# Unnormalised tap diagonals, a later request of chunk 1, and a split evacuation in the start-up of a fused convolution and gated MLP kernel

## The chip, the cores and the metric

The kernel runs on one core of one Trainium2 chip. The metric is device time in microseconds (us). Where runs are compared with each other, they were run in the same rounds on the same chip as the kernel before.

Engine names in the profile: PE is TensorE (PEld its weight loads), ACT is ScalarE, DVE is VectorE, POOL is GpSimd, SP is SyncE. A name with a "q" at the end (SPq, POOLq) is the sequencer of that engine, here issuing a DMA.

Other terms: a tap is one of the seven weights of the convolution, or the operation that applies it. A diagonal is the identity matrix times one tap; with it PE applies that tap in a matmul. A group is 64 of the 192 channels in both batch halves, on 128 partitions. PSUM holds what matmuls write, SBUF the other tiles; an evacuation is the copy from PSUM to SBUF. Fillers are matmuls on zeros whose results nobody reads.

## The reference

```python
# x [8, 4096, 192], weight [8 heads, 7 taps]
w = softmax(weight, axis=-1)                    # per head
x_pad = zeros(6 rows) ++ x                      # causal, along the sequence
conv[b, s, h, g] = sum_k w[h, k] * x_pad[b, s + k, h, g]
# MLP on 32768 tokens: w_in [192, 2048], w_out [2048, 192], beta [2048]
h = conv @ w_in
out = (h * sigmoid(beta * h)) @ w_out           # fp32 out
```

The kernel computes SiLU(beta*h), which is beta times too large, and divides the output weights by beta once, at start-up.

## The kernel before

The sequence is worked in 32 chunks of 1024 tokens (512 tokens in each of two batch halves). In steady state, PE multiplies hidden and output layers without a pause, VectorE computes the convolution of chunk s+2 with seven tap operations, and ScalarE does the SiLU. Only chunks 0 and 1 are handled specially, because nothing has run ahead of them. That start-up is what the change touches.

SyncE issues the loads in this order; `load_x(x1, ...)` is chunk 1, `w_in_raw` are the first 256 columns of the input weights in fp32, needed for the first two hidden tiles:

```python
    for i in range(2):
        load_x(x0, 0, i)                       # chunk 0, two halves
    load_x(x1, TOK, 0)                         # chunk 1, first half
    for r in range(2):
        nc.sync.dma_start(out=w_in_raw[r * DG : (r + 1) * DG], in_=w_in_v[:, :, 0:F0])
    load_x(x1, TOK, 1)                         # chunk 1, second half
    for i in range(NW - 1):
        load_w_out(i)                          # output weights, fp32, slices 0 to 2
    load(2)
    load_w_out(NW - 1)
    load(3)
```

The tap weights, their diagonals (for the convolution of groups 0 and 1 of chunk 0 on PE), and GpSimd's loads of the other input-weight columns. The traces show these loads in the software queue (q0); they cast fp32 to bf16 on the way, and I call them the casting loads. The one-element copy `hold` keeps them back until the taps are ready:

```python
    nc.vector.reduce_max(nmax, pw, axis=mybir.AxisListType.X, negate=True)
    nc.scalar.activation(cw, pw, AF.Exp, bias=nmax, accum_out=total)
    nc.scalar.activation(warm, warm, AF.Silu)
    nc.vector.reciprocal(total, total)
    nc.vector.tensor_scalar_mul(cw, cw, total)
    # ... (cut)
    for b in range(NB):
        cast_rows(nc.vector.tensor_copy, x0b, x0, b)
        if b == 1:
            diags(0, 2)
    hold = setup.tile([1, 1], FP32)
    nc.gpsimd.tensor_copy(hold, cw[0:1, 0:1])
    load_w_in(F0, FW)                          # casting loads, two DMAs each
    for i in range(1, NW):
        load_w_in(i * FW, (i + 1) * FW)
```

The evacuation of the four transposed blocks of chunk 0, and the rest that matters here:

```python
    for b in range(NB):
        # ... transposes of block b into pt (cut)
        (nc.vector.tensor_copy if b == 2 else nc.scalar.copy)(tokens(xt0, b), pt)
        # ... (cut)
    diags(2, 4)
    diags(4, K)
    # ... per group c of chunk 0: seven matmuls; ScalarE casts chunk 1, evacuates
    #     group c, and casts w_in_raw to bf16 after group 0 (cut)
    # ... group 2: five taps on VectorE, two on PE, added (cut)
    scale_w_out(0)                             # output-weight slice / beta, on GpSimd
    scale_w_out(1)                             # GpSimd too; slices 2 and 3 on VectorE
    # ... (cut)
    first_work = {                             # VectorE's work in step u of chunk 0
        4: [None, None],                       # None: one tap operation of chunk 1
        5: [None],
        6: [conv1_evac, lambda: scale_w_out(2), None],
        # ... (cut)
    }
```

## Time and profile before

| | before |
|---|---|
| time, median of the 3 runs at first, of 6 beside the change | 690.03, 690.42 us |
| profiled span | 688.0 us |
| PE busy | 682.2 us |
| first convolution matmul | 7.21 us |
| first hidden matmul | 11.12 us |
| first hidden matmul of chunk 1 | 29.39 us |

The profile page, the line of busy times and the chain of work that ended last:

```profile
PE 682.2 (99%) x11312; PEld 521.1 (76%) x11312; DVE 524.7 (76%) x467; ACT 579.0 (84%) x530; POOL 9.9 (1%) x20
...
PE 98%; DMA 1%; ACT 0%; DVE 0%; issue 0%; ACTq 0%
```

PE is the limit, and the kernel can gain or lose only where PE has to wait: in the first 30 us.

The timeline of the kernel before (start in us, duration in us, engine, source line, operation, output and inputs, count; in brackets the idle time before it and what ended it):

```profile
0.81 1.48 SPq L158 DMA_DIRECT2D x<-in_x_dram  x3
...
2.34 1.31 SPq L169 DMA_DIRECT2D w_in_raw<-in_moe_w_in_dram  x2
...
3.69 0.60 SPq L158 DMA_DIRECT2D x<-in_x_dram  x1
...
4.29 5.24 POOL L211 DMA_DIRECT2D w_in_s<-in_moe_w_in_dram  x8
...
7.68 0.48 DVE L338 TENSOR_SCALAR ct<-xt,cw 128x512 bf16<-128x512 f32 x1
...
9.62 0.83 ACT L332 CAST w_in_s<-w_in_raw 128x768 bf16<-128x768 f32 x1
...
11.12 1.66 PE L424 MATMUL ph<-ct,w_in_s 64*128 64x512 bf16 x12
...
11.42 0.69 DVE L352 TENSOR_TENSOR ct<-pa,ct 128x512 bf16<-128x512 f32 x1
...
15.39 1.69 DVE L338 TENSOR_SCALAR ct<-xt,cw 128x1024 bf16<-128x1024 bf16 x1
...
29.39 0.83 PE L424 MATMUL ph<-ct,w_in_s 64*128 64x512 bf16 x6
```

The last line is my landmark: from there PE runs without a pause, so a shift of this line is a shift of the end.

Two more views of the kernel before. First, the loads of `w_in_raw` alone (issues, and the time from issue to landing); the two DMAs, issued at 2.34 and 3.05, landed at 7.87 and 8.75:

```profile
L169 SPq DMA_DIRECT2D w_in_raw<-in_moe_w_in_dram x2: 597/635/673, 2.3 to 3.1; - x2
...
DMA to landing us min/median/max: 5.5/5.6/5.7
```

### The profile page before, as it was taken

How to read it: one execution, taken by the hardware profiler on the slowest of the kernel's cores; microseconds unless marked ns; L12 is line 12 of the kernel's file. 1: busy time of each engine (PE TensorE's matmuls, PEld its weight loads, DVE VectorE, ACT ScalarE, POOL GpSimd, SP SyncE). 2: the span in 40 equal slices, each digit the busy share in tenths (PEclk: the TensorE clock that was granted, in tenths of full speed). 3: DMA queues.
4: the chain of work that ended last, by engine and by line, in shares of the span. 5: the costliest groups of instructions: out<-in, count | busy, mean ns of one | idle time of the engine just before them, and what ended most of it. 6: DMA issues, size and time to landing. Idle time of an engine off the chain costs nothing.

```text
span 688.0 us, 24344 instructions
## 1 busy us (share of the span) xinstructions
PE 682.2 (99%) x11312; PEld 521.1 (76%) x11312; DVE 524.7 (76%) x467; ACT 579.0 (84%) x530; POOL 9.9 (1%) x20
## 2 busy tenths in 40 slices
PE   8999999999999999999999999999999999999998
PEld 4777777777777777777777777777777777777777
DVE  7989877788777787777797777887777977777712
ACT  7988888888888888888888888888888888888893
POOL 5000000000000000000000000000000000000000
PEclk9999999999999999999999999999999999999999
DMA  9734333244332244332444332444323443322111
GB/s 234 190 97 117 105 100 98 58 107 117 101 99 77 77 116 116 95 99 61 98 117 105 93 97 57 116 117 96 103 60 93 117 109 96 100 59 59 49 36 59
DMA packets 121861, 67.06 MB, mean 97 GB/s; under 512 B 53264, under 2 KB 121760, under 8 KB 121760
## 3 DMA queue, kind: packets, MB, share of 16 engines
q1 hardware_dynamic: 120048, 64.12, 34.7%
q0 software_dynamic: 1664, 1.38, 1.2%
q8 instruction: 88, 1.44, 0.9%
q14 instruction: 13, 0.11, 0.0%
q10 hardware_dynamic: 48, 0.01, 0.0%
HBM read 29.89 MB, written 25.17 MB: 80 GB/s over the span
## 4 chain that ended last, share of the span: by engine, by line
PE 98%; DMA 1%; ACT 0%; DVE 0%; issue 0%; ACTq 0%
PE ph L424 48%; PE pa L457 25%; PE pb L457 24%; DMA x<-in_x_dram 1%; PE pb L287 1%; ACT g L432 0%; PE ph L287 0%; DVE x0b L226 0%; ACT xt L302 0%; PE pa L287 0%; PE pb L233 0%; PE ph L233 0%; DVE diag L260 0%; ACT osb L473 0%; ACT beta L309 0%
## 5 line engine op out<-in xcount | busy, mean ns | idle before, releaser
L432 ACT ACTIVATE g<-ph,beta 128x1024 bf16<-128x1024 f32 x512 | 569.7, 1115 | 94.5 <-PE ph L424 89.8
L457 PEld LDWEIGHTS <-g 64*128 64x128 bf16 x8160 | 370.7, 94 | 102.3 <-issue 0.2
L424 PE MATMUL ph<-ct,w_in_s 64*128 64x512 bf16 x3072 | 424.3, 376 | 0.9 <-ACT g L432 0.9
L340 DVE SCALAR_TENSOR_TENSOR ct<-xt,cw,ct 128x1536 bf16<-128x1536 bf16 (+2 forms) x190 | 336.9, 1773 | 2.5
L457 PE MATMUL pa<-w_out_s,g 64*128 64x192 bf16 x4112 | 244.8, 243 | 0.0
L457 PE MATMUL pb<-w_out_s,g 64*128 64x192 bf16 (+1 forms) x4048 | 230.4, 243 | 0.0
L424 PEld LDWEIGHTS <-w_in_s 64*128 64x128 bf16 x3072 | 159.6, 94 | 54.8 <-issue 2.7
L475 DVE TENSOR_REDUCE osb<-pa 128x384 f32<-128x768 f32 x64 | 61.3, 958 | 122.5 <-PE pa L457 121.1
L475 DVE TENSOR_REDUCE osb<-pb 128x384 f32<-128x768 f32 x63 | 60.3, 957 | 29.1 <-PE pb L457 29.1
L106 DVE CAST xb<-xf 128x768 bf16<-128x768 f32 x60 | 40.5, 677 | 0.0
L338 DVE TENSOR_SCALAR ct<-xt,cw 128x1536 bf16<-128x1536 bf16 (+2 forms) x32 | 32.4, 1011 | 0.0
L473 ACT COPY osb<-pb 128x192 f32<-128x192 f32 x1 | 0.3, 319 | 7.2 <-PE pb L457 7.2
L211 POOL DMA_DIRECT2D w_in_s<-in_moe_w_in_dram x8 | 5.2, 662 | 0.0
L223 PE MATMUL ph<-zeros 128*128 128x512 bf16 (+2 forms) x11 | 4.1, 485 | 1.1 <-DVE warm L180 1.1
L287 PE MATMUL pb<-xt,diag 64*128 64x512 f32 (+1 forms) x21 | 4.7, 443 | 0.0
L121 DVE COPY xt<-xt 128x18 bf16<-128x18 bf16 x27 | 4.4, 164 | 0.0
L287 PEld LDWEIGHTS pb<-xt,diag 64*128 64x128 f32 (+1 forms) x21 | 2.7, 187 | 0.9 <-issue 0.4
L314 POOL TENSOR_TENSOR w_out_s<-w_out_raw,beta_r 128x768 bf16<-128x768 f32 x2 | 3.1, 1564 | 4.1 <-DVE beta_r L354 3.2
L223 PEld LDWEIGHTS <-zeros 128*128 128x128 bf16 x11 | 1.2, 121 | 2.2 <-issue 1.1
L181 ACT ACT_TABLE_LOAD x1 | 1.3, 1283 | 1.8 <-PEq L593 1.8
L226 ACT CAST x1b<-x 128x384 bf16<-128x384 f32 x3 | 2.0, 714 | 0.4 <-DMA x<-in_x_dram 0.4
L287 PE MATMUL ph<-xt,diag 128*128 128x512 f32 x7 | 1.9, 409 | 0.1
(55 smaller groups left out, 26.9 us busy)
## 6 DMA issues: line engine op xcount, KB each, us to landing
out_dram<-osb SPq DMA_DIRECT2D x127, 192.0 KB, 2.2
xf<-in_x_dram SPq DMA_DIRECT2D x60, 384.0 KB, 4.3
xt<-xb SPq DMA_TRANSPOSE x120, 2.6
x<-in_x_dram SPq DMA_DIRECT2D x4, 384.0 KB, 4.9
w_out_raw<-in_moe_w_out_dram SPq DMA_DIRECT2D x4, 384.0 KB, 13.5
w_in_s<-in_moe_w_in_dram POOLq DMA_DIRECT2D x6, 192.0 KB, 10.5
w_in_raw<-in_moe_w_in_dram SPq DMA_DIRECT2D x2, 192.0 KB, 5.6
w_in_s<-in_moe_w_in_dram POOLq DMA_DIRECT2D x2, 96.0 KB, 7.4
```

What stands on the lines that cost most here:

```text
L106: nc.vector.tensor_copy(xbs[ch][:, :, :, h, :], xfs[ch][:, h].rearrange("q b (p c) -> q b c p", c=NG),)
L121: nc.vector.tensor_copy(dst, last[:, :, HALO + TOK - PAD :])
L211: nc.gpsimd.dma_start(out=w_in_s[r * DG : (r + 1) * DG, :, c0:c1], in_=w_in_v[:, :, c0:c1])
L223: nc.tensor.matmul(pf[:, 0, 0:cols], zeros, zc, start=True, stop=True)
L287: nc.tensor.matmul(pv, diag[rows, k, :], xt[rows, o : o + TOK], start=(k == k0), stop=(k == K - 1),)
L314: (nc.vector if i > 1 else nc.gpsimd).tensor_tensor(w_out_s[:, fcs, :], w_out_raw[:, fcs, :], beta_r[:, fcs].unsqueeze(2).to_broadcast((12 ...
L338: nc.vector.tensor_scalar_mul(dst, src, scalar)
L340: nc.vector.scalar_tensor_tensor(out=dst, in0=src, scalar=scalar, in1=dst, op0=ALU.mult, op1=ALU.add)
L424: nc.tensor.matmul(ph[:, h, :], w_in_s[rows, j, fc * 128 : (fc + 1) * 128], cts[s][rows, j, :], start=(j == 0), stop=(j == NG - 1),)
L432: nc.scalar.activation(gs[s][:, fc], ph, AF.Silu, scale=beta[:, fc : fc + 1])
L457: nc.tensor.matmul(self.po[:, r, b * D : (b + 1) * D], g[rows, fc, self.h, q * BLK : (q + 1) * BLK], w_out_s[rows, fc, :], start=(self.don ...
L475: nc.vector.tensor_reduce(dst, self.po[:, :, 0 : nb * D].rearrange("p r n -> p n r"), axis=mybir.AxisListType.X, op=ALU.add,)
```

## The change

The intent: take two small VectorE operations (reciprocal, scaling) out of the path to the first diagonals by building them from the unnormalised exponentials `eu`, and apply the normalisation `rn` where results leave PSUM; give chunk 0 the DMA engines to itself by requesting chunk 1 only when the taps have arrived; let the first convolution start when group 0 of the last two blocks has been evacuated; and move one slice of output-weight scaling from GpSimd to VectorE.

The one-element memset into `x1` is the gate of the second part: SyncE's load into that buffer has to wait for it, and it stands behind `reduce_max` in VectorE's queue. Everything behind it in SyncE's program waits as well: in the trace after the change the memset ran at 3.19, chunk 1 was requested at 3.30 and w_in_raw at 3.71.

```diff
     for i in range(2):
         load_x(x0, 0, i)
-    load_x(x1, TOK, 0)
-    for r in range(2):
-        nc.sync.dma_start(out=w_in_raw[r * DG : (r + 1) * DG], in_=w_in_v[:, :, 0:F0])
-    load_x(x1, TOK, 1)
-    ... the loads behind them (cut)
@@
     nc.vector.reduce_max(nmax, pw, axis=mybir.AxisListType.X, negate=True)
-    nc.scalar.activation(cw, pw, AF.Exp, bias=nmax, accum_out=total)
+    nc.scalar.activation(eu, pw, AF.Exp, bias=nmax, accum_out=total)
     nc.scalar.activation(warm, warm, AF.Silu)
-    nc.vector.reciprocal(total, total)
-    nc.vector.tensor_scalar_mul(cw, cw, total)
+    nc.vector.memset(x1[0:1, 0, 0, 0, 0:1], 0.0)
+    load_x(x1, TOK, 0)
+    for r in range(2):
+        nc.sync.dma_start(out=w_in_raw[r * DG : (r + 1) * DG], in_=w_in_v[:, :, 0:F0])
+    load_x(x1, TOK, 1)
+    ... the loads behind them (cut)
@@  diags() multiplies by eu instead of cw
+    diags(0, 4)
     for b in range(NB):
         cast_rows(nc.vector.tensor_copy, x0b, x0, b)
         if b == 1:
-            diags(0, 2)
+            diags(4, K)
@@
-    nc.gpsimd.tensor_copy(hold, cw[0:1, 0:1])
+    nc.gpsimd.tensor_copy(hold, eu[0:1, 0:1])
@@
-        (nc.vector.tensor_copy if b == 2 else nc.scalar.copy)(tokens(xt0, b), pt)
+        copy = nc.vector.tensor_copy if b == 2 else nc.scalar.copy
+        for cs in (slice(0, 1), slice(1, NG)) if b > 1 else (slice(0, NG),):
+            copy(tokens(xt0, b)[:, cs], pt[:, cs])
@@
-    diags(2, 4)
-    diags(4, K)
+    nc.vector.reciprocal(rn, total)
+    nc.vector.tensor_scalar_mul(cw, eu, rn)
@@
-        (nc.vector if i > 1 else nc.gpsimd).tensor_tensor(
+        (nc.vector if i else nc.gpsimd).tensor_tensor(     # scale_w_out
@@  evacuations
-        nc.scalar.copy(cts[0][:, c, :], pv[:, 0, :])
+        nc.scalar.mul(cts[0][:, c, :], pv[:, 0, :], rn)
-    nc.vector.tensor_tensor(dst, pv, dst, ALU.add)
+    nc.vector.scalar_tensor_tensor(
+        out=dst, in0=pv, scalar=rn, in1=dst, op0=ALU.mult, op1=ALU.add
+    )
-            nc.vector.tensor_copy(cts[1][rows, 0, :], pv[rows, r, :])
+            nc.vector.tensor_scalar_mul(cts[1][rows, 0, :], pv[rows, r, :], rn[rows])
@@
     scale_w_out(0)
-    scale_w_out(1)
@@
-        4: [None, None],
+        4: [None, lambda: scale_w_out(1), None],
```

More of the change, by code (lines that the diff above doesn't have):

```diff
@@ L166 @@
         load_x(x0, 0, i)
-    load_x(x1, TOK, 0)
-    for r in range(2):
-        nc.sync.dma_start(out=w_in_raw[r * DG : (r + 1) * DG], in_=w_in_v[:, :, 0:F0])
-    load_x(x1, TOK, 1)
-    for i in range(NW - 1):
-        load_w_out(i)
-    load(2)
-    load_w_out(NW - 1)
-    load(3)
     zeros = setup.tile([128, 128], BF16)
@@ L247 @@
     total = setup.tile([128, 1], FP32)
+    rn = setup.tile([128, 1], FP32)
     cw = consts.tile([128, K], FP32)
+    eu = setup.tile([128, K], FP32)
     nc.vector.reduce_max(nmax, pw, axis=mybir.AxisListType.X, negate=True)
-    nc.scalar.activation(cw, pw, AF.Exp, bias=nmax, accum_out=total)
+    nc.scalar.activation(eu, pw, AF.Exp, bias=nmax, accum_out=total)
     nc.scalar.activation(warm, warm, AF.Silu)
-    nc.vector.reciprocal(total, total)
-    nc.vector.tensor_scalar_mul(cw, cw, total)
+    nc.vector.memset(x1[0:1, 0, 0, 0, 0:1], 0.0)
[3 more added lines that the diff above has]
+    load_x(x1, TOK, 1)
+    for i in range(NW - 1):
+        load_w_out(i)
+    load(2)
+    load_w_out(NW - 1)
+    load(3)
     beta = consts.tile([128, NF], FP32)
@@ L262, in diags @@
             ident.unsqueeze(1).to_broadcast((128, k1 - k0, 128)),
-            cw[:, k0:k1].unsqueeze(2).to_broadcast((128, k1 - k0, 128)),
+            eu[:, k0:k1].unsqueeze(2).to_broadcast((128, k1 - k0, 128)),
             ALU.mult,
         )
+    diags(0, 4)
     for b in range(NB):
```

## The prediction

> **What bounds the kernel now.** TensorE: the page gives PE 682.2 us busy of a 688.0 us span (99%); the chain that ended last is 98% PE, and the windows show PE 100% busy from 15 to 680 us. The change removes no steady matmul. Only a shift of PE's start-up (the first 15 us) can move the time, so the ceiling is small.
>
> **The start-up before (timeline, chain of waits):** the first half of chunk 0 lands at 4.38 us; VectorE casts it, builds diagonals 0-1 (0.41 us) and casts the second half (landed 5.45) from 5.49 to 6.22; PE transposes; ScalarE evacuates block 3 (0.50 us, to 7.16); first convolution matmul at 7.21. PE then runs 16 convolution and 8 hidden matmuls and is held once more: group 2's hidden matmuls start at 12.16, right behind VectorE's last add (11.42-12.11), though PE's pitch of 0.215 us would have had them at 11.99. VectorE's taps (7.69 to 11.31) set that add; PE's part was ready at 11.18. Then two SiLUs pace PE until 14.82.
>
> **The change, costed.**
> 1. Unnormalised diagonals start at 3.67 instead of waiting for 4.10. From 0.41 us (2 taps) and 0.55 (3), 4 taps take 0.69 us (estimate), to about 4.36, just when chunk 0 lands: hidden. Diagonals 4-6 (0.55) replace 0.41 us between the casts, so the later casts run about 0.08 us late.
> 2. Split evacuation: ScalarE's first group takes about 0.26 us instead of 0.50 (estimate from 0.17 at 16 columns and 0.50 at 384). But PE's own filler lasts to 7.11 and the first convolution waits for it too, so at most 0.06 us shows, which the later casts eat. First convolution: 7.2, unchanged. The Trainium skill ("VectorE: DVE Perf Modes", the section on the TRN2 errata) says each instruction pays a fixed cost; VectorE's two pieces should take about 0.65 us against 0.56.
> 3. Between the block-2 copy and the taps VectorE loses two diagonal builds (0.88 us together) and gets reciprocal and scaling (0.16 + 0.23, plus a wait). Taps start near 7.5 instead of 7.69, the add ends near 11.95, group 2 starts near 12.0. This is the gain: about 0.15 us.
> 4. Chunk 1 is requested at about 3.4 instead of 1.8 us. Chunk 0's second half lands near 5.1, before VectorE is ready. Chunk 1 and followers stay within 0.5 us of their old landings (7.56; 7.87, 8.75; 9.68), because chunk 0 keeps the DMA engines busy until about 4.5. The Trainium skill ("DMA: Bandwidth & Descriptors", "Issuing engines are not separate DMA queues") says all issues share 16 engines: reordering adds no bandwidth.
> 5. VectorE instead of GpSimd scales the second slice of output weights (0.95 us, was 1.66). Chunk 1's first tap, beside GpSimd, took 1.69 us; alone about 0.7 (estimate from 1.00 at 1536 columns). Neutral. VectorE's last tap ended 29.26, its consumer ran at 29.60: slack 0.3 us.
> 6. Normalisation in the evacuations: same passes, no gain.
>
> **Prediction:** 689.9 us (before 690.03), range 689.2 to 690.7. Chances: faster by over 2% 0.005, within 2% 0.99, slower 0.005.
>
> **Right if** the first convolution stays at 7.1-7.3, the taps begin near 7.5, group 2 near 12.0, and total PE busy is unchanged. **Wrong if** chunk 1 or the first input weights land over 0.8 us later (hidden matmuls after 11.2); if the second output-weight slice lands after 16.1 and stalls VectorE so that chunk 1's taps end after 29.6; or if the casts start clearly earlier because chunk 0 lands earlier (gain to 0.5 us).

## More of the kernel before

All hardware loads that the start-up needs (three of x, two of w_in_raw, and the last of x at 3.69) are issued before GpSimd issues its first casting load at 4.29.

The waits of the first 25 us that a DMA ended were short (engine and line, what it waited for, us in total, times, longest):

```profile
POOL w_out_s L314 <- DMA w_out_raw<-in_moe_w_out_dram: 1.0, 1, 1.0
...
ACT x1b L226 <- DMA x<-in_x_dram: 0.4, 1, 0.4
...
DVE x0b L226 <- DMA x<-in_x_dram: 0.3, 1, 0.3
```

Second, the DMA traffic between 6 and 9 us, by queue (q1 is SyncE's hardware queue, q0 the software queue; the last number is the share of the 16 engines' time):

```profile
DMA packets 651, 0.74 MB, mean 246 GB/s; under 512 B 41, under 2 KB 651, under 8 KB 651
...
q1 hardware_dynamic: 651, 0.74, 101.4%
```

There is no q0 line: the casting loads had been issued from 4.29 us on, and not one of their packets moved in these 3 us. Their first packet starts at 9.56.

## The result, and the profile after

The changed kernel took 695.35 us, median of 6 runs (694.69 to 695.98), against 690.42 us (689.92 to 691.13) for the kernel before in as many runs. The ratio is 1.0071, with a 95% interval of 1.0058 to 1.0084: about 4.9 us slower, and outside my range. A ratio is the mean time of one kernel's fast runs over that of the other's fast runs of the same rounds, so it is not quite the ratio of the medians quoted. By the 2% rule the verdict is "same", but the loss is well clear of the noise.

The page after (line numbers of the changed kernel differ by a few from those before):

```profile
PE 684.0 (99%) x11312; PEld 521.0 (75%) x11312; DVE 525.5 (76%) x469; ACT 579.3 (84%) x531; POOL 8.8 (1%) x19
...
PE 95%; DMA 2%; DVE 2%; SPq 0%; issue 0%; ACT 0%
```

DMA and VectorE have entered the chain that ended last. The timeline after:

```profile
0.81 2.85 SPq L158 DMA_DIRECT2D x<-in_x_dram  x3
...
3.71 1.31 SPq L250 DMA_DIRECT2D w_in_raw<-in_moe_w_in_dram  x2
...
4.35 5.31 POOL L202 DMA_DIRECT2D w_in_s<-in_moe_w_in_dram  x8
...
5.06 0.61 SPq L158 DMA_DIRECT2D x<-in_x_dram  x1
...
7.62 0.49 DVE L344 TENSOR_SCALAR ct<-xt,cw 128x512 bf16<-128x512 f32 x1
...
11.39 0.75 DVE L358 SCALAR_TENSOR_TENSOR ct<-pa,rn,ct 128x512 bf16<-128x512 f32 x1
13.35 0.83 ACT L338 CAST w_in_s<-w_in_raw 128x768 bf16<-128x768 f32 x1 [3.35 <-DMA w_in_raw<-in_moe_w_in_dram]
...
14.24 1.82 PE L431 MATMUL ph<-ct,w_in_s 64*128 64x512 bf16 x12 [2.89 <-ACT w_in_s L338]
...
19.84 0.48 DVE L344 TENSOR_SCALAR ct<-xt,cw 128x1024 bf16<-128x1024 bf16 x1
...
21.82 0.96 DVE L320 TENSOR_TENSOR w_out_s<-w_out_raw,beta_r 128x768 bf16<-128x768 f32 x1 [1.50 <-DMA w_out_raw<-in_moe_w_out_dram]
...
34.30 0.40 PE L431 MATMUL ph<-ct,w_in_s 64*128 64x512 bf16 x2
34.94 0.61 PE L431 MATMUL ph<-ct,w_in_s 64*128 64x512 bf16 x4 [0.24 <-DVE ct L346]
```

Two things stand out. The load of x at 5.06 is now issued behind the first casting load at 4.35, and so is the second load of w_in_raw (issued at 4.42, inside the 3.71 line). And ScalarE sits idle for 3.35 us until w_in_raw has landed; PE's first hidden matmul moves from 11.12 to 14.24. The landmark moves from 29.39 to 34.30, and once more by 0.4 us within that tile, where PE waits for VectorE's last tap (34.94; at the old pitch, 0.21 us behind the first matmul, it would be 34.51). Together that is 5.3 us, and the span grew from 688.0 to 693.3. So the whole loss lies before 35 us.

The loads of w_in_raw:

```profile
L250 SPq DMA_DIRECT2D w_in_raw<-in_moe_w_in_dram x2: 597/633/669, 3.7 to 4.4; - x2
...
DMA to landing us min/median/max: 4.1/6.5/8.8
```

The first, issued at 3.71, landed at 7.86, as before (7.87). The second, issued at 4.42, landed at 13.27 (before: 8.75). Chunk 1's second half landed at 14.92 (before: 9.68). The traffic from 6 to 9 us after:

```profile
DMA packets 500, 0.45 MB, mean 151 GB/s; under 512 B 37, under 2 KB 500, under 8 KB 500
...
q1 hardware_dynamic: 364, 0.39, 48.3%
q0 software_dynamic: 136, 0.07, 22.8%
```

Now the software queue moves data in this window (first packet at 6.20), and the sum is 151 GB/s instead of 246. The hardware queue moved 0.39 MB instead of 0.74. The two shares add to 71%, so the engines were not even full.

The waits for DMAs, after:

```profile
POOL w_out_s L320 <- DMA w_out_raw<-in_moe_w_out_dram: 8.3, 1, 8.3
ACT w_in_s L338 <- DMA w_in_raw<-in_moe_w_in_dram: 3.3, 1, 3.3
...
DVE x1b L217 <- DMA x<-in_x_dram: 2.8, 1, 2.8
...
DVE w_out_s L320 <- DMA w_out_raw<-in_moe_w_out_dram: 1.5, 1, 1.5
```

The last of them is a second loss. VectorE now scales an output-weight slice in the middle of chunk 1's taps. That slice landed at 21.80 instead of 15.07, and the taps stand behind it.

One more thing in the trace is not a cause. PE's granted clock was 0.5 from 15.53 to 18.95 us. The Trainium skill ("TensorE: Matmul & The Clock Gate", "What's actually happening") says that the clock gate watches free-running windows of about 3.4 us and halves the clock after an idle one. The trace agrees on the length: the slow stretch lasted 3.41 us. It does not agree on the idle window: of the 3.41 us before the clock fell, PE was idle for 2.1 us and busy for the rest. The repeat of this kernel (below) had no slow stretch at all and took the same time (694.92 us).

### The profile page after: what moved, and what is told of

The parts are those of the page before. It is cut to its first block, busy times and chain, and to the rows that moved or that the text cites. A ratio compares the mean times of both kernels' runs of the same rounds, so it can differ in the third digit from the quotient of the medians.

```text
span 693.3 us, 24349 instructions
## 1 busy us (share of the span) xinstructions
PE 684.0 (99%) x11312; PEld 521.0 (75%) x11312; DVE 525.5 (76%) x469; ACT 579.3 (84%) x531; POOL 8.8 (1%) x19
## 4 chain that ended last, share of the span: by engine, by line
PE 95%; DMA 2%; DVE 2%; SPq 0%; issue 0%; ACT 0%
PE ph L431 46%; PE pa L464 24%; PE pb L464 24%; DMA w_out_raw<-in_moe_w_out_dram 2%; DVE ct L346 1%; DVE w_out_s L320 0%; PE ph L214 0%; DVE ct L410 0%; SPq L250 0%; DVE xb L106 0%; SPq L158 0%; PE pa L235 0%; SPq L148 0%; ACT osb L480 0%; DVE nmax L242 0%
## 5 line engine op out<-in xcount | busy, mean ns | idle before, releaser
L320 DVE TENSOR_TENSOR w_out_s<-w_out_raw,beta_r 128x768 bf16<-128x768 f32 x3 | 2.9, 953 | 1.5 <-DMA w_out_raw<-in_moe_w_out_dram 1.5
```

Of the source, the lines that this page charges most:

```text
L320: (nc.vector if i else nc.gpsimd).tensor_tensor(w_out_s[:, fcs, :], w_out_raw[:, fcs, :], beta_r[:, fcs].unsqueeze(2).to_broadcast((128, N ...
```

## The experiments

Theory 1: the gate itself is harmless, but it pushes two loads that the start-up needs behind the first casting load; loads issued behind casting loads share the DMA engines with them and land some 5 us late. Theory 2: the late request lets the hardware queue run short of work at about 5 us, and that is the cost, whatever GpSimd loads. Theory 3: the loss is in VectorE's new work. Kernels are compared only within the same rounds.

| run | what it is | time, us | ratio to before (95%) | second w_in_raw lands | chunk 1 on PE |
|---|---|---|---|---|---|
| before | | 690.42 | 1 | 8.75 | 29.39 |
| change | | 695.35 | 1.0071 (1.0058-1.0084) | 13.27 | 34.30 |
| e1_no_gate | change, no gate | 691.53 | 1.0015 (1.0002-1.0028) | 10.28 | 30.25 |
| e2_gate_alone | before, gate only | 694.13 | 1.0051 (1.0037-1.0064) | 12.69 | 33.75 |
| e3_pool_scale | change, slice on GpSimd | 693.53 | 1.0042 (1.0026-1.0057) | 13.64 | 34.59 |
| e4_sw_late | change, casting loads later | 692.02 | 1.0026 (1.0012-1.0039) | 9.69 | 31.50 |
| e5_sw_early | before, casting loads earlier | 692.91 | 1.0038 (1.0023-1.0054) | 10.89 | 32.40 |
| e6_w_in_first | change, w_in_raw ahead of the gate | 690.42 | 1.0000 (0.9987-1.0014) | 8.20 | 30.10 |
| e7_slice_alone | before, slice on VectorE | 690.14 | 1.0000 (0.9987-1.0012) | 9.49 | 29.65 |
| e8_diag_evac | diagonals and evacuation only | 691.06 | 1.0011 (0.9999-1.0024) | 9.71 | 29.88 |
| e9_change_again | the change | 694.92 | 1.0065 (1.0051-1.0079) | 12.57 | 34.64 |
| e10_pool_scale_again | as e3 | 693.15 | 1.0042 (1.0027-1.0057) | 12.24 | 32.55 |
| e11_no_cast | change, loads without cast, wrong result | 702.42 | one run | 15.70 | 42.11 |
| e12_w_in_first_reordered | as e6, ScalarE reordered | 690.85 | 1.0012 (1.0000-1.0025) | 8.16 | 29.71 |

The last two columns are in us, from the one profiled execution of each.

### e1_no_gate: the change without the gate

```diff
-    nc.vector.memset(x1[0:1, 0, 0, 0, 0:1], 0.0)
```

> The change without the one-element memset into chunk 1's buffer, so that nothing holds SyncE and the loads are issued at about 1.8 to 4.3 us as before. Everything else of the change stays. If the late request is the whole loss (theories 1 and 2): second first-columns input-weight load lands at 8.5 to 9.0 (was 13.27 with the change), chunk 1's second half at 9.5 to 10, hidden matmuls start at 11.1 to 11.2, time 689.5 to 690.3, slightly under before. If VectorE's new work (theory 3: output-weight slice, longer diagonals) is the loss, it stays above 693.

Measured: 691.53 us, ratio 1.0015. With SyncE's loads issued at 1.83 to 3.70 as before, the first hidden matmul came at 11.26. So removing one memset of one element brings back about four of the five microseconds, and theory 3 fails as the main cause. But the run was still about 1 us slower than before, not slightly faster: the landings were later than I expected (10.28 and 11.24), and PE then waited 0.4 us for a casting load. With the same order of issue the second w_in_raw load landed at 8.75 before, 9.49 in e7 and 9.71 in e8, so this landing varies by 1.5 us for reasons that stay open.

### e2_gate_alone: the kernel before with only the gate

```diff
-    load_x(x1, TOK, 0)  and all the loads behind it (moved down)
@@
     nc.scalar.activation(cw, pw, AF.Exp, bias=nmax, accum_out=total)
+    nc.vector.memset(x1[0:1, 0, 0, 0, 0:1], 0.0)
+    load_x(x1, TOK, 0)  and all the loads behind it
```

> The kernel before with the late request alone (loads moved behind the maximum, memset in front); GpSimd still scales two output-weight slices. Theories 1 and 2: second input-weight load lands after 12.5, hidden matmuls start near 14, time 692.5 to 695. Theory 3: 690.0 to 690.7, as before.

Measured: 694.13 us, ratio 1.0051, first hidden matmul at 13.65. The gate alone costs about 3.5 us in a kernel with none of the other parts. Both halves, taking it away and adding it alone, agree. They do not yet tell theory 1 from theory 2.

### e4_sw_late: the change, with the casting loads issued later

```diff
-    nc.gpsimd.tensor_copy(hold, eu[0:1, 0:1])
+    nc.gpsimd.tensor_copy(hold, x0b[0:1, NB - 1, 0, 0, 0:1])
```

> The change, but GpSimd's casting loads of the input weights wait for chunk 0's last cast (about 6.2 us) instead of the exponentials (3.6), so all of the four loads that start-up needs are issued ahead of them. Theory 1 (the needed loads were slowed because they were queued behind the first casting loads and share the engines with them): second input-weight load back to about 9, chunk 1's second half to about 10, hidden matmuls near 11.2, time 690 to 691.5 (the casting loads themselves may now come late, needed at about 13.8). Theory 2 (the engines ran dry at 4.5 to 5.5 and the late request itself costs the 5 us, whatever GpSimd loads): still 13, time 694 to 696.

The gate is kept, so SyncE issues as late as in the change, and only GpSimd's loads move (first issue 6.38). The loads of w_in_raw in this run (the time from issue to landing):

```profile
DMA to landing us min/median/max: 4.2/4.7/5.3
```

And PE's wait for the casting loads, from the view of waits:

```profile
PE ph L431 <- DMA w_in_s<-in_moe_w_in_dram: 1.1, 2, 0.6
```

The longest time from issue to landing falls from 8.8 to 5.3 us; the second load lands at 9.69 and the first hidden matmul comes at 11.61. Theory 2 said 13 and fails: the request is as late as in the change, yet once the casting loads stand behind it, the landings are only about 1 us later than before the change (9.69 and 10.77, against 8.75 and 9.68). The time, 692.02 us, is 0.5 us above what I expected, because the casting loads themselves are now late and PE waits for them.

### e5_sw_early: the kernel before, with the casting loads issued earlier

```diff
-    nc.gpsimd.tensor_copy(hold, cw[0:1, 0:1])
+    nc.gpsimd.tensor_copy(hold, ident[0:1, 0:1])
```

> The kernel before, nothing of the change, but GpSimd's casting loads are released by the identity matrix (ready at about 2.3 us) instead of the tap weights (4.1). SyncE's loads are issued at the old times, so the queue does not run dry; yet the second input-weight load (issued 3.05) and chunk 1's second half (3.69) now stand behind casting loads. Theory 1 (order against the casting loads): the second input-weight load lands after 11 (was 8.75), chunk 1's second half after 12.5 (was 9.68), hidden matmuls start after 12, time 692 to 695. Theory 2 (the late request leaves the engines dry): landings as before, 690 to 691.

This is the mirror of e4: there is no gate, SyncE issues at the old times, and GpSimd's first issue moves from 4.29 to 2.47, ahead of the second w_in_raw load (3.06). The DMA traffic from 6 to 9 us in this run:

```profile
DMA packets 629, 0.48 MB, mean 159 GB/s; under 512 B 37, under 2 KB 629, under 8 KB 629
...
q1 hardware_dynamic: 349, 0.34, 55.1%
q0 software_dynamic: 280, 0.14, 43.6%
```

And the two loads of w_in_raw, from issue to landing:

```profile
DMA to landing us min/median/max: 6.8/7.3/7.8
```

Measured: 692.91 us, ratio 1.0038, so 2.6 us are lost with nothing of the change in the kernel. The software queue is in the window again, and the rate is 159 GB/s, nearly as low as with the change. Here the two shares add to 98.7%: the engines were not short of work, but the software queue moved only 0.14 MB in its 43.6% of their time. The second w_in_raw load landed at 10.89 (I had said after 11), chunk 1's second half at 13.58, and the first hidden matmul came at 11.87, a little under the 12 that I had set. The first of these figures is weak evidence, as the same load landed at 10.28 in e1 with the old order; chunk 1's second half (11.24 in e1) and the time carry the finding. The direction is theory 1's, and theory 2 fails again. The loss has a different route here: PE later waited 1.4 us for the second output-weight slice, which GpSimd could only scale after its late landing at 21.19.

### e6_w_in_first: the change, with w_in_raw loaded ahead of the gate

```diff
     for i in range(2):
         load_x(x0, 0, i)
+    for r in range(2):
+        nc.sync.dma_start(out=w_in_raw[r * DG : (r + 1) * DG], in_=w_in_v[:, :, 0:F0])
@@
     nc.vector.memset(x1[0:1, 0, 0, 0, 0:1], 0.0)
     load_x(x1, TOK, 0)
-    for r in range(2):
-        nc.sync.dma_start(out=w_in_raw[r * DG : (r + 1) * DG], in_=w_in_v[:, :, 0:F0])
     load_x(x1, TOK, 1)
```

> The change with one reordering: the two input-weight loads go ahead of the gate, so only chunk 1 waits for it. All four needed loads are then issued by about 4.1, just ahead of the first casting load (4.35). Theory 1: input-weight loads land by 9, chunk 1's second half by 11, hidden matmuls near 11.2 to 11.5, time 690.5 to 692 (like the run without the gate, whose 1 us over before comes from elsewhere). Theory 2: the first landings are still some us late, 693 or more.

Measured: 690.42 us, ratio 1.0000. Chunk 1 is still requested behind the taps, at 3.30 and 3.83, but both requests now come before the first casting load at 4.35. The loads of w_in_raw:

```profile
L168 SPq DMA_DIRECT2D w_in_raw<-in_moe_w_in_dram x2: 597/633/669, 1.8 to 2.5; - x2
...
DMA to landing us min/median/max: 5.5/5.6/5.7
```

They land at 7.32 and 8.20, chunk 1's second half at 10.21. The first hidden matmul came at 11.85, later than the 11.2 to 11.5 that I had expected, because ScalarE waited 1.7 us for chunk 1 before it cast w_in_raw; the time was a little under my range all the same. Two lines of SyncE's order undo the whole loss (to within the interval, 0.9987 to 1.0014), with the gate, the diagonals, the evacuation and the slice all in place.

### e7_slice_alone and e8_diag_evac: the other parts

e7 is the kernel before with `scale_w_out(1)` on VectorE, as in the change:

```diff
-        (nc.vector if i > 1 else nc.gpsimd).tensor_tensor(
+        (nc.vector if i else nc.gpsimd).tensor_tensor(
@@
-    scale_w_out(1)
@@
-        4: [None, None],
+        4: [None, lambda: scale_w_out(1), None],
```

> The kernel before with the second output-weight slice on VectorE, and nothing else. The run without the gate was 1 us over before, and its trace shows PE waiting for a casting load at 16.0 to 16.8 and VectorE for the slice at 16.0. If the slice on VectorE is what costs that microsecond: 691.2 to 692. If not (I lean to this, as VectorE's tap should shrink from 1.69 to about 0.5): 690.0 to 691.0, within 0.3 us of before.

Measured: 690.14 us, ratio 1.0000. By itself the slice on VectorE costs nothing that these rounds can see (interval 0.9987 to 1.0012), as predicted.

e8 is the change without the gate and with the slice back on GpSimd:

```diff
-    nc.vector.memset(x1[0:1, 0, 0, 0, 0:1], 0.0)
@@
-        (nc.vector if i else nc.gpsimd).tensor_tensor(
+        (nc.vector if i > 1 else nc.gpsimd).tensor_tensor(
@@
+    scale_w_out(1)
@@
-        4: [None, lambda: scale_w_out(1), None],
+        4: [None, None],
```

> The change without the gate and without the slice on VectorE: the unnormalised diagonals, the normalisation in the evacuations and the split evacuation alone. If these start VectorE's taps earlier as predicted: 689.7 to 690.4. If they are what costs the microsecond (VectorE's longer work beside GpSimd at 3.7 to 4.4 us, casting loads landing 1.2 us later): 691.2 to 692.

Measured: 691.06 us, ratio 1.0011, interval 0.9999 to 1.0024. This is inconclusive on a cost of about 0.8 us, but it leaves little room for the gain that I had predicted: the group 2 matmuls started at 12.25, not at 12.0 (12.16 before).

### e3, e9 and e10: what the slice costs beside the late loads

e3 and e10 are the same kernel: the change with `scale_w_out(1)` back on GpSimd. e9 is the change itself.

```diff
-        (nc.vector if i else nc.gpsimd).tensor_tensor(
+        (nc.vector if i > 1 else nc.gpsimd).tensor_tensor(
@@
+    scale_w_out(1)
@@
-        4: [None, lambda: scale_w_out(1), None],
+        4: [None, None],
```

> The change with the second output-weight slice given back to GpSimd. The hidden matmuls still start near 14.2 (3.1 us late), but VectorE's taps of chunk 1 no longer stand behind a slice that lands at 21.8. If that queueing adds to the loss: 693.0 to 694.5, 1 to 2 us faster than the change. If not, it equals the change, 695.3.

Measured: 693.53 us, ratio 1.0042. Its trace could not be used beside that of the change: the profiled execution was the slowest of four (694.89), and in it PE's product with the tap weights, and with it the gate, came 0.5 us late (chunk 1 was requested at 3.80).

> The change itself, unaltered, on the same chip and in the same rounds as the next run, to have the two beside each other: 694.7 to 696, ratio to before near 1.007, as before. Its trace should again show the second input-weight load after 12.5 us and hidden matmuls near 14.

> The change with the second output-weight slice back on GpSimd, again, beside the change: its first trace fell on the slowest of four runs, in which the gate itself came 0.5 us late. If VectorE's place in the queue behind a late slice is worth what the two ratios say (1.0071 against 1.0042): 1.3 to 2.3 us under the run beside it. If it was the chip: within 0.7 us of it.

Measured: 694.92 us and 693.15 us, ratios 1.0065 and 1.0042. So 1.8 us of the loss go away with the slice on GpSimd (every run of e9 was slower than every run of e10, 693.85 or more against 693.31 or less), although the same slice cost nothing in e7. VectorE's timeline in e9:

```profile
17.78 0.48 DVE L344 TENSOR_SCALAR ct<-xt,cw 128x1024 bf16<-128x1024 bf16 x1
22.17 0.96 DVE L320 TENSOR_TENSOR w_out_s<-w_out_raw,beta_r 128x768 bf16<-128x768 f32 x1 [3.91 <-DMA w_out_raw<-in_moe_w_out_dram]
23.04 2.60 DVE L346 SCALAR_TENSOR_TENSOR ct<-xt,cw,ct 128x1024 bf16<-128x1024 bf16 x2
```

And in e10:

```profile
18.54 0.48 DVE L344 TENSOR_SCALAR ct<-xt,cw 128x1024 bf16<-128x1024 bf16 x1
19.06 2.61 DVE L346 SCALAR_TENSOR_TENSOR ct<-xt,cw,ct 128x1024 bf16<-128x1024 bf16 x2
```

In e9 VectorE stands idle for 3.91 us in front of a slice that has not landed, with chunk 1's taps ready to run behind it. In e10 the taps go on at once, and GpSimd, which has nothing else to do, takes the wait. The landmark is 34.64 in e9 and 32.55 in e10.

### e11_no_cast: is it the cast?

```diff
-                out=w_in_s[r * DG : (r + 1) * DG, :, c0:c1], in_=w_in_v[:, :, c0:c1]
+                out=w_in_x[r * DG : (r + 1) * DG, :, c0:c1], in_=w_in_v[:, :, c0:c1]   # fp32 scratch
@@
-                    w_in_s[rows, j, fc * 128 : (fc + 1) * 128],
+                    w_in_s[rows, j, fc % 2 * 128 : (fc % 2 + 1) * 128],
```

> Wrong result on purpose. The change, with GpSimd's loads at their old times but without the cast: they write fp32 into a scratch tile that nobody reads, and the hidden layer reads the first 256 columns over and over. Only landings before 15 us count. If it is the cast that slows the loads queued behind: second input-weight load lands by 10.5 us. If any GpSimd-issued load ahead of it does so: after 12 us again. I lean to the second at 0.6.

The result was wrong, and the total (702.42 us, one run) says nothing. The second w_in_raw load landed at 15.70, later than in the change. So the cast is not needed to slow the loads behind it; GpSimd's loads without a cast, which write twice the bytes, do it too. Because of these bytes, the run does not tell whether the cast adds anything of its own.

### e12_w_in_first_reordered: a candidate to beat both

In e6 ScalarE waited 1.7 us for chunk 1 before it did what PE needed. This run lets it cast w_in_raw and evacuate group 0 first, and gives half of chunk 1's casts to VectorE.

```diff
         if c == 0:
-            for b in range(2):
-                cast_rows(nc.scalar.copy, x1b, x1, b)
+            nc.scalar.copy(w_in_s[:, :, 0:F0], w_in_raw)
         nc.scalar.mul(cts[0][:, c, :], pv[:, 0, :], rn)
-        if c == 0:
-            nc.scalar.copy(w_in_s[:, :, 0:F0], w_in_raw)
-    cast_rows(nc.scalar.copy, x1b, x1, 2)
+        cast_rows(nc.scalar.copy, x1b, x1, c)
@@
-    cast_rows(nc.vector.tensor_copy, x1b, x1, 3)
+    for b in range(2, NB):
+        cast_rows(nc.vector.tensor_copy, x1b, x1, b)
```

> A candidate to beat both: the change with the input-weight loads ahead of the gate, ScalarE casting those weights and evacuating group 0 before it touches chunk 1 (which held ScalarE 1.7 us in that run's trace), and VectorE taking half of chunk 1's casts. Hidden matmuls should start at 11.1 to 11.4 instead of 11.85, group 2 near 12.1, chunk 1's first hidden matmul at 29.3 to 29.8 against 30.1. Time 689.6 to 690.3, ratio 0.999 to 1.000; a gain over before of more than 0.5 us would surprise me.

Measured: 690.85 us, ratio 1.0012, interval 1.0000 to 1.0025. It beats the change but not the kernel before. Its five runs spread from 690.13 to 692.17. In its trace chunk 0's second half landed at 5.84 and the first hidden matmul came at 11.56, so the miss began ahead of what I had reordered. No version that I ran is faster than the kernel before.

## Why the prediction was wrong

**Step 4 failed, and the whole loss follows from it.** I wrote: "Chunk 1 and followers stay within 0.5 us of their old landings (7.56; 7.87, 8.75; 9.68), because chunk 0 keeps the DMA engines busy until about 4.5." The first two did: 7.14 and 7.86. The next two landed at 13.27 and 14.92, late by 4.5 and 5.2 us, and the hidden matmuls started at 14.24, the first thing that I had listed under "wrong if". I had asked only whether the hardware queue would run dry. I had not asked which other queue's loads would come to stand in front. The first casting load is issued at 4.3 us in both kernels; a shift of 1.5 us moved two of SyncE's loads from one side of that moment to the other. e4 and e5 show that it is this order: with the gate kept, moving GpSimd's loads back restores the landings to within about 1 us, and without any gate, moving them forward spoils them. e6 shows that the order can be mended without giving up the late request.

I had cited the Trainium skill's statement that all issues share 16 engines and interleave, and concluded that reordering "adds no bandwidth". That was half of it: the order also took bandwidth away, 246 to 151 GB/s between 6 and 9 us. Why the sum falls in this stretch stays open. Two active queues alone do not bring it so low: from 10 to 15 us of the kernel before both were active, and the rate was 232 to 243 GB/s. Nor is it mere bytes in front: the one casting load issued ahead of the second w_in_raw load carries 96 KB, 0.7 us at 151 GB/s (my estimate), against a delay of 4.5 us. e11 shows that the cast is not needed for the late landings. So the order is shown to be the cause, and how it delays them is not.

**Step 5 was right alone and wrong in company.** "Neutral" is what e7 measured (1.0000): the slice took 0.96 us on VectorE, and chunk 1's first tap fell from 1.69 to 0.48 us once GpSimd no longer worked beside it (I had estimated 0.7). But with the slice landing near 22 us instead of 15.07 it holds up VectorE, and that is worth 1.8 us (e9 against e10). I had named this among the things that would make me wrong ("if the second output-weight slice lands after 16.1"), and did not see that step 4 would bring it about.

**Step 3's gain of 0.15 us did not come in this trace.** In the change the taps began at 7.62 (before 7.69; I said 7.5), and the last add ended at 12.14 (before 12.11; I said 11.95). In e8, without the gate, group 2 started at 12.25. Two terms were off. PE's fillers ran on to 5.29 us (before to 4.88), so the transposes and the evacuations behind them came later than VectorE's casts alone would have them; the first record of a full clock is at 5.29 us in the change and at 4.33 before. And the add with the factor takes 0.75 us instead of 0.69. The repeat, e9, whose clock was full from 4.81, shows the head start: the first convolution at 7.19, the taps from 7.38, the last add ended at 12.02. So 0.1 us of this gain can be there in one execution and not in another, and behind the late weights it could not show in the time.

**Step 2** had the first convolution at 7.2; it was 7.42, it seems for the same reason (7.19 in e9). The sizes were right: ScalarE's first group took 0.27 us (I said 0.26), and VectorE's two pieces 0.62 against 0.56 for one (I said 0.65), which agrees with the fixed cost per instruction that I cited (the table of that section has such a term for reads of PSUM too, as here).

**Step 1** was right: diagonals 0 to 3 ran from 3.67 to 4.36 us, hidden behind chunk 0's landing.

**Step 6** ("same passes, no gain") was right that nothing would be gained, but the change was not free: ScalarE's evacuation with a factor took 0.69 us against 0.59 for the plain copy. The Trainium skill ("ScalarE: Activation LUTs", "What ACT_TABLE_LOAD costs") says that each per-partition pointer operand adds about 93 ns; the trace agrees (0.10 us more).

**What the sum looks like.** Gate alone 3.5 us (e2); gate with diagonals and evacuation 2.9 us (e10); with the slice on VectorE as well 4.5 us in the same rounds, 4.9 in the first ones. e2 and e10 have overlapping intervals, so the difference between them is not a finding. The 0.8 us over before of e8, the 1.0 us of e1 and the 0.8 us of e12 are at the edge of what these rounds resolve, and e6, which contains the same diagonals and evacuation, measured none. Whether these parts cost something is not settled.

## What to carry to other kernels

Before delaying a DMA, list every other queue's issues in order of time, and ask which of them will now stand in front of it: here 1.5 us of delay became 5 us because two urgent loads fell behind the first of eight bulk loads of another engine. Put urgent loads ahead of bulk ones across all queues, not only within one, and hold back the bulk ones if something must wait. An operation that waits for a late DMA belongs on an engine with nothing else to do; on the engine that paces the next stage, it turns a late landing into lost time, and a test of that part alone will not show it.

## What the Trainium skill lacked or had wrong

- "DMA: Bandwidth & Descriptors", "Queues, rings and completion order", says that each engine takes turns between the queue rows it has work for, at packet granularity. In the kernel before no software packet moved for 5.3 us after the first casting load was issued (4.29 to 9.56), while the hardware queue kept the engines busy (101.4% from 6 to 9 us). The delay was 1.85 us in the change, 4.7 in e4, 3.5 in e5 and 4.1 in e6. In all 14 traces the first software packet moved when the hardware queue had moved 80 to 112% of the bytes issued to it before the first software load (1250 of 1344 KB in the change, 1146 of 1344 in e5, 2505 of 2688 in e4). Whether the software queue had its descriptors ready before that, the traces do not show. The page has nothing on such an order between the queues, nor on how late it can make the first byte (its "Latency and other measured facts" gives about 1 us for software DMAs).
- The same page has no number for a hardware load that is issued just behind a software one: from issue to landing it took 8.8 us in the change against 5.7 before, and the sum of both queues fell from 246 to 151 GB/s between 6 and 9 us, with the engines 71% busy (159 GB/s at 98.7% in e5).
- "SBUF — State Buffer", "Who interferes with whom", describes the lock between VectorE and GpSimd; of how much an operation can grow it gives two ratios (6.8 and 1.5), without the operations' sizes. Here GpSimd's one-element copy took 0.70 instead of 0.17 us while VectorE built the diagonals, VectorE's 18-column halo copy 1.18 instead of 0.16 us beside GpSimd's scaling, and a 1024-column tap 1.69 instead of 0.48.
- "TensorE: Matmul & The Clock Gate", "What's actually happening", has the clock halve after a window of about 3.4 us in which PE is idle. Here it halved after windows of 3.41 us in which PE was idle for 2.1 us (the change) and 2.0 us (e3) only, and did not after 1.9 us (e2 and e9).
